# The end of an attention loop rearranged: one matmul group put back among the slots, casts moved to VectorE, gate sums moved into the loop

## The chip, the cores and the metric

The kernel runs on one core of a Trainium2 chip. The metric is the device time of the whole launch in microseconds, the median of several runs: 732.4 us before the change (three runs, 732.12 to 733.97 us). The profile is of one further execution, which took 732.09 us.

## The reference

With x of 2048 tokens by 512 features, everything in float32:

```python
g = sigmoid((x * gate_w).sum(-1, keepdims=True))      # one gate per token
q, k, v = x @ wqkv                                    # 32 heads of 16
p = softmax(mask(q @ k.T * 16 ** -0.5))               # causal, window of 256 keys
a = (p @ v) @ wo
b = (sigmoid(x @ w_gate) * (x @ w_up)) @ w_down       # hidden width 1376
return g * a + (1 - g) * b
```

## The kernel before, in words

Float32 products are made from parts. A value is split into a high part (a cast to the float32r type) and a low part (value minus high part), and a product is three matmuls: high by high, high by low, low by high. So each operand costs one cast (ScalarE, the function `split`, L84, and its relatives at L128 and L613) and one subtraction (VectorE, L85, L129, L614).

**First stretch, the attention loop.** The 32 heads form 8 groups of 4, a group has 16 blocks of 128 tokens, so there are 128 units (NU). The loop over `u` runs for N = 140 units, because a unit's later parts lag behind its first. In unit u the scores of block u are computed only for their row maxima (`s_part`, L338 on TensorE, L344 on VectorE, while u < 128), the transposed scores of block u - 9 are computed and exponentiated (`st_part`, L388 on TensorE, L393 on ScalarE, while u - 9 < 128), GpSimd masks them (`mask_p`, L398 and L403), and in some even units a burst of small matmuls multiplies probabilities by values (`pv_burst`, L442). The last bursts come in units 130, 132, 134, 136 and 138. What a burst gives is copied by ScalarE (L456), added to by VectorE (L459, `rest` in `o_take`) and stored to DRAM scratch, four stores of outputs and one of the softmax sums.

Between these parts stand **slots**. The generator `turns` walks through groups of 12 matmul steps: projections for later units, then the products with the gate and up weights (`gu_mm`, L271). A slot issues two half-height matmuls: step t of the chain on rows 0 to 63 and step t - 19 of the chain (SHIFT = 19) on rows 64 to 127. With G groups the chain has 12 G + 19 steps, of which the first and last 19 issue one half only. When a group ends, ScalarE copies it out of PSUM into a buffer with the tag `sp` (L548, four buffers), and its store to the scratch `gu_scratch` is queued. `run_slots(n)` takes n slots; the tables GAPS and LAST say how many follow each head hh, and LAST serves for u >= 128.

HOLD groups are left out of the chain and run at the end on the full array, 12 matmuls in one go (`hold_group`). Before the change HOLD is 1: the last group, up-projection chunk 10 for tokens 1536 to 2047, runs at the head of unit 138.

**Second stretch, the steps.** 44 steps n = (c, f), 4 token chunks of 512 by 11 hidden chunks, accumulate the down-projection: 4 token tiles by 3 matmuls, 12 in all (`pd`, L88 to L90). The third of each three (L90) needs the low part of the hidden values, the first needs the high part. After the last f of a chunk, 48 matmuls of the output projection (`pa`) follow, and the gate combines the two. The hidden values of a step are loaded from scratch five steps ahead (`h_load`, L627, two transfers of 256 KB), then `h_skew(n)` splits those of step n + 2 (L84, L85; tiles `hb`) and makes those of step n + 3 (sigmoid on ScalarE, L639; multiplication on VectorE, L640). `h_skew(-3)` to `h_skew(-1)` stand at the ends of units 136 to 138. There are seven buffers for loaded hidden values; those of steps 5 and 6 lie in memory that holds probabilities which the burst of unit 138 reads.

**What sets the order.** It is written out by hand: every engine works through its instructions in program order, and all transfers are issued by one queue, that of SyncE (called SPq in the profile), also in order. The lists `acts` and `behind` hold small jobs: after each head's matmuls one job of `behind` and one of `acts` is issued; a job of `acts` is a cast that puts its subtraction into `behind`. The list `later` holds stores that are issued at the head of the next unit. From unit 138 on (`u >= N - 2`) both lists are emptied at the end of the unit.

Other jobs at the loop's end: the down weights (`load_d`, `split_d`, tiles `wdraw` to `ring`), loaded every second unit from WD = 123 and split two units later; the output weights (`wo_split`, tiles `woraw` to `xh`, `xl`), put into `acts` in unit 136; and the inverses of the softmax sums (`sums_load`, L649, and `sums_invert`, L653), of which the fourth is loaded in unit 139 and inverted in step 2.

**The gate sums.** `z_load` loads a block of 128 tokens of x (tile `zx`, tag `sp`), `z_sum` multiplies it by the broadcast gate weights (`zw`) and sums along the row (L803). For the first chunk of tokens the loads stand in steps 0 and 1 and the sums in steps 2, 8 and 10.

Of the kernel before, what the change touches and what calls it, by code (L numbers as in the profile page):

```python
# [7 lines left out]
F32 = mybir.dt.float32  # L8
# [3 lines left out]
ALU = mybir.AluOpType  # L12
# [35 lines left out]
PVLAG = LAG + 2  # L48
SD = 3
QB = 32  # L50
HOLD = 1
GAP = 3
GAP0 = (4, 3, 5)
SHIFT = 19
GAPS = ((3, 3, 3, 3), (3, 2, 3, 0), (3, 3, 3, 3), (3, 2, 3, 2))
LAST = (3, 2, 3, 2)
WD_LATE = {0: 9, 2: 10}
WD_SPLIT = {0: 7, 1: 8, 3: 9, 5: 10}
AHEAD = 5


# [1 line left out]
def gated_mix_kernel(  # L63
# [60 lines left out]
    def split_d(f, late=False):  # L124
        fw = FCH[f]
        dh, dl = ring_f(f)
        hi, lo, raw = dh[0:fw], dl[0:fw], raw_d.pop(f)[0:fw]
        nc.scalar.copy(hi, raw)  # L128
        low = lambda: nc.vector.tensor_tensor(lo, raw, hi.bitcast(F32), op=ALU.subtract)  # L129
        behind.append(low) if late else low()  # L130

# [4 lines left out]
    with ExitStack() as actx:  # L136
# [473 lines left out]
            wo_raw.extend(raw[:, d] for d in range(2))  # L610

        def wo_split(d):
            nc.scalar.copy(wo_h[d], wo_raw[d])  # L613
            behind.append(lambda: nc.vector.tensor_tensor(  # L614
                wo_l[d], wo_raw[d], wo_h[d].bitcast(F32), op=ALU.subtract))

# [9 lines left out]
            for w in range(2):  # L626
                nc.sync.dma_start(hvs[n % NHV][0:FCH[f], w], gu_d[w, f, 0:FCH[f], c * CH:(c + 1) * CH])  # L627

        def h_skew(n):
            a, b = n + 2, n + 3  # L630
            if 0 <= a < len(steps):
                fw = FCH[steps[a][1]]
                hts[a] = cpool.tile([P, CH2], F32R, tag="hb", name=f"hb{a}", bufs=4)
                src = hvs[a % NHV][0:fw, 1]
                split(hts[a][0:fw, 0:CH], hts[a][0:fw, CH:], src)
            if 0 <= b < len(steps):
                fw = FCH[steps[b][1]]
                tg, tu = hvs[b % NHV][0:fw, 0], hvs[b % NHV][0:fw, 1]
                nc.scalar.activation(tg, tg, AF.Sigmoid)  # L639
                nc.vector.tensor_tensor(tu, tg, tu, op=ALU.mult)  # L640
# [16 lines left out]
            for _ in range(n):  # L657
                next(slots, None)

        def hold_group(step, _, post):  # L660
            for k in range(3 * ND):
                step(k)
            post()

        n_rest = len(work) + len(rest) + NSTEP - 8 - HOLD
        N = NU + PVLAG + 1
        SUMS = NU - 13 + PVLAG + 1
        U_LAST = 4 * (NSTEP - 2 - 5)
        HLOAD = N - 2 * AHEAD
        WD = NU - 5  # L670
        WO = NU - 8
        slots = turns()
        bursts = {}
        w = 0
# [6 lines left out]
        for u in range(N):  # L681
# [22 lines left out]
            later.clear()  # L704
            run_dmas(sdma[:SD])
            del sdma[:SD]
            if u in (WO, WO + 2):
                wo_load((u - WO) // 2)
            if u == N - 4:
                acts.extend(lambda d=d: wo_split(d) for d in range(ND))  # L710
            if WD <= u < WD + 18 and (u - WD) % 2 == 0:
                load_d((u - WD) // 2)
# [2 lines left out]
                s4 = (u + 2) // 4 + 4  # L715
            if s4 is not None:
                work.append(proj_group(s4))
            if u >= NU + PVLAG - HOLD and rest:
                hold_group(*rest.pop(0))
            for hh in range(HG):  # L720
                if hh == 0 and u % 2 == 0:
                    if u in bursts:
# [27 lines left out]
                        split_wqk(g, r, 0), behind.append(lambda: split_wqk(g, r, 1))))  # L750
            if 0 <= u - LAG < NU:
                mask_p(u - LAG)
            if WD + 2 <= u < WD + 16 and (u - WD) % 2 == 0:
                acts.append(lambda f=(u - WD) // 2 - 1: split_d(f, True))
            if SUMS <= u and (u - SUMS) % 4 == 0:
                sums_load((u - SUMS) // 4)
# [1 line left out]
                behind.append(lambda c=(u - SUMS) // 4: later.append(sums_invert(c)))  # L758
            if u >= HLOAD and (u - HLOAD) % 2 == 0:
                h_load((u - HLOAD) // 2)  # L760
            if u >= N - 2:
                flush(acts)
                flush(behind)
            if u >= N - 4:
                run_dmas(later)
                later.clear()
                if u < N - 1:
                    h_skew(u - N + 1)
        assert not (work or behind or acts or raw_gu or sdma or obs)

        def slot(h, d, c):
# [15 lines left out]
        wide = [blocks(spare[k][:, 2]) for k in range(2)]  # L787
        rows = [blocks(free_slot(0, k, 3)) for k in range(2)]
        accs = [spare[k % 2][:, k // 2] for k in range(4)]

        zx = {}
        zj = {}
        zw = cpool.tile([P, CH], F32, tag="ob", name="zw", bufs=2)
        nc.sync.dma_start(zw, gw.partition_broadcast(P).rearrange("p o f -> p (o f)"))

        def z_load(b):
            zx[b] = cpool.tile([P, CH], F32, tag="sp", name=f"zx{b}", bufs=4)
            nc.sync.dma_start(zx[b], x[b * P:(b + 1) * P, :])

        def z_sum(b, c):  # L800
            if c not in zj:
                zj[c] = ps.tile([P, D], F32, tag="st", name=f"zj{c}", bufs=3)
            nc.vector.tensor_tensor_reduce(  # L803
                zj[c], zx.pop(b), zw, scale=1.0, scalar=0.0, op0=ALU.mult, op1=ALU.add,
                accum_out=gsum[:, b:b + 1],
            )

        def gate(c):
            b = slice(4 * c, 4 * c + 4)
# [19 lines left out]
        for n, (c, f) in enumerate(steps):  # L829
            fw = FCH[f]  # L830
            if n + AHEAD < len(steps):
                h_load(n + AHEAD)
            h_skew(n)
            if n in WD_LATE:
                load_d(WD_LATE[n])
            if n in WD_SPLIT:
                split_d(WD_SPLIT[n])
            if f == 0:
                pd = [
                    ps.tile([P, D], F32, tag="s" if t < 2 else "st", name=f"pd{4 * c + t}", bufs=2 + t // 2)  # L840
                    for t in range(4)
                ]
            if n in (0, 1):
                z_load(2 * n)
                z_load(2 * n + 1)
            for b in {2: (0, 1), 8: (2,), 10: (3,)}.get(n, ()):
                z_sum(b, 0)
            if f == 8 and c + 1 < NC:
                for t in range(4):
                    z_load(4 * c + 4 + t)  # L850
            if f == NF - 1:
                gate(c)
            if n == 2:
                last_sums = sums_invert(NC - 1)
            if n == 3:
                nc.sync.dma_start(*last_sums)
            if 1 <= f < 9 and f % 2 == 1:
                o_load(4 * c + f // 2)
            if 3 <= f and f % 2 == 1:
                o_scale(4 * c + f // 2 - 1)  # L860
            if 4 <= f and f % 2 == 0:
                o_split(4 * c + f // 2 - 2)
            dh, dl = ring_f(f)
            hb = hts.pop(n)
            for t in range(4):
                ts = slice(t * P, (t + 1) * P)
                mm3(pd[t], hb[0:fw, ts], hb[0:fw, CH:][:, ts], dh[0:fw], dl[0:fw], f == 0, f == NF - 1)
            if f < NF - 1:
                continue
            for t in range(4):  # L870
                b = 4 * c + t
                acc = accs[b % len(accs)]
                nc.scalar.activation(acc, pd[t], AF.Copy, scale=omg[:, b:b + 1])
                pa = ps.tile([P, D], F32, tag="misc", name=f"pa{b}", bufs=3)
                for d in range(ND):
                    mm3(pa, oh[t][:, d], ol[t][:, d], wo_h[d], wo_l[d], d == 0, d == ND - 1)
                nc.vector.scalar_tensor_tensor(
                    acc, pa, gs[:, b:b + 1], acc, op0=ALU.mult, op1=ALU.add,
                )
                nc.sync.dma_start(out[b * P:(b + 1) * P, :], acc)  # L880
                if c + 1 < NC:
                    z_sum(b + 4, c)


_INS = ["xT", "wqk", "wv", "wo", "wgu", "wgu_last", "wg_last", "wd", "gw", "x"]
# [51 lines left out]
```

## Time and profile before

| what | value |
|---|---|
| time, median of three runs | 732.4 us |
| time of the profiled execution | 732.09 us |
| its span (first to last instruction) | 730.4 us |
| TensorE busy | 720.5 us, 99% |
| VectorE, ScalarE busy | 471.1 us, 436.8 us |
| TensorE's granted clock | 1.00 |
| bytes moved | 117.13 MB, mean 160 GB/s |

The span is 1.7 us shorter than the time of its execution; what lies around it is taken as fixed. The unit loop ends near 557 us of the span, where the burst of unit 138 ends; the 44 steps fill the rest. In rows of the timeline the columns are: start in us, duration in us, engine, line, operation, output and inputs, and in square brackets the idle time of the engine before it and who ended it. In rows of the chain they are start, duration, and what. Matmuls overlap: a full-width one is shown with 0.39 us, while the next starts 0.23 us after it.

### The profile page before, as it was taken

Reading aid. Unit: us, or ns where it says so; the run is one execution under the profiler, and the core shown is the slowest. Engines: PE = TensorE matmul, PEld = TensorE weight load, DVE = VectorE, ACT = ScalarE, POOL = GpSimd, SP = SyncE. Lnnn points to the kernel's source line nnn. Section 1 sums busy time; section 2 is a strip of 40 time slices with the busy share of each in tenths; the row PEclk is TensorE's granted clock in tenths of the full one; section 3 lists DMA queues with packets and bytes.
Section 4 is the critical chain, followed back from the end, with each engine's and each line's share of the span. In section 5 each row is a group of like instructions: output and inputs, shape, how many; then the busy total and the mean of one; then the engine's idle time right before and its main releaser. Section 6 shows DMA issues by size and latency. Waiting matters only on the chain.

```text
span 730.4 us, 20456 instructions
## 1 busy us (share of the span) xinstructions
PE 720.5 (99%) x7759; PEld 591.8 (81%) x7759; DVE 471.1 (65%) x1460; ACT 436.8 (60%) x899; POOL 166.8 (23%) x256
## 2 busy tenths in 40 slices
PE   9999999999999999999999999999999899999997
PEld 7688888888878878888787888888876688888886
DVE  5335766776676776767677676676426788577571
ACT  6412676677577666767667776766777455435241
POOL 7000332233223323323323323332321000000000
PEclk9999999999999999999999999999999999999999
DMA  9356455454355445445434635554466979567441
GB/s 321 98 155 205 121 134 150 140 144 127 121 137 149 132 136 142 131 136 136 136 115 139 160 86 150 166 151 153 124 203 177 304 260 274 185 228 244 155 131 58
DMA packets 88426, 117.13 MB, mean 160 GB/s; under 512 B 33294, under 2 KB 43150, under 8 KB 88328
## 3 DMA queue, kind: packets, MB, share of 16 engines
q1 hardware_dynamic: 88328, 115.83, 53.5%
q8 instruction: 61, 1.00, 0.6%
q14 instruction: 37, 0.30, 0.1%
HBM read 54.17 MB, written 36.45 MB: 124 GB/s over the span
## 4 chain that ended last, share of the span: by engine, by line
PE 93%; SPq 2%; DMA 2%; DVE 1%; ACT 1%; issue 0%; DVEq 0%; ACTq 0%
PE gu L271 36%; PE pj L271 10%; PE pvs L442 8%; PE st L388 6%; PE s L338 6%; PE pd L90 5%; PE pd L88 5%; PE pd L89 5%; PE vps L253 3%; PE pa L88 2%; PE pa L90 2%; PE pa L89 2%; SPq L313 2%; PE pvst L442 2%; PE gl L486 1%; PE vps L88 1%
## 5 line engine op out<-in xcount | busy, mean ns | idle before, releaser
L344 DVE CUSTOM_DVE_ANT_0 junk<-s,mask 128x384 f32<-128x384 f32 (+2 forms) x512 | 267.4, 531 | 150.7 <-PE st L388 89.3
L271 PE MATMUL gu<-xh,w 64*128 64x512 f32 x1280 | 337.2, 395 | 0.0
L393 ACT ACTIVATE region<-st 128x384 f32<-128x384 f32 (+2 forms) x512 | 241.7, 476 | 91.9 <-PE st L388 44.5
L271 PE MATMUL gu<-xl,w 64*128 64x512 f32 x640 | 228.9, 393 | 0.0
L271 PEld LDWEIGHTS gu<-xh,w 64*128 64x128 f32 x1280 | 190.5, 185 | 17.9 <-issue 5.5
L398 POOL TENSOR_SCALAR_AFFINE_SELECT region<-region 128x512 f32<-128x512 f32 x128 | 85.5, 668 | 367.0 <-ACT region L393 334.8
L388 PE MATMUL st<-ring 64*128 64x384 f32 (+2 forms) x536 | 168.1, 322 | 1.0 <-ACT region L393 0.6
L338 PE MATMUL s<-ring 64*128 64x384 f32 (+2 forms) x536 | 167.6, 321 | 0.3 <-DVE mx L344 0.3
L271 PEld LDWEIGHTS gu<-xl,w 64*128 64x128 f32 x640 | 115.0, 185 | 4.5
L338 PEld LDWEIGHTS s<-ring 64*128 64x128 f32 x536 | 98.6, 184 | 22.7 <-DVE mx L344 12.2
L388 PEld LDWEIGHTS st<-ring 64*128 64x128 f32 x536 | 98.3, 184 | 8.8 <-ACT region L393 1.9
L271 PE MATMUL pj<-xl,wqh 64*128 64x512 f32 (+1 forms) x240 | 95.5, 402 | 0.0
L271 PE MATMUL pj<-xh,wqh 64*128 64x512 f32 (+1 forms) x240 | 93.5, 394 | 0.0
L271 PE MATMUL pj<-xh,wql 64*128 64x512 f32 (+1 forms) x240 | 75.3, 392 | 0.0
L442 PE MATMUL pvs<-region,vg 64*32 64x320 f32 (+4 forms) x1440 | 73.4, 345 | 0.0
L90 PE MATMUL pd<-ring,hb 128*128 128x512 f32 (+1 forms) x176 | 69.4, 394 | 2.7 <-DVE hb L85 2.7
L403 POOL TENSOR_SCALAR_AFFINE_SELECT region<-region 128x512 f32<-128x512 f32 x112 | 71.9, 642 | 0.0
L442 PE MATMUL pvst<-region,vg 64*32 64x320 f32 (+4 forms) x1440 | 71.7, 340 | 0.0
L88 PE MATMUL pd<-ring,hb 128*128 128x512 f32 (+1 forms) x176 | 69.3, 394 | 0.7 <-ACT hb L84 0.7
L89 PE MATMUL pd<-ring,hb 128*128 128x512 f32 (+1 forms) x176 | 68.6, 390 | 0.0
L442 PEld LDWEIGHTS pvs<-region,vg 64*32 64x32 f32 x1440 | 45.2, 106 | 26.0 <-issue 5.5
L84 ACT CAST hb<-region 128x512 fp32r<-128x512 f32 (+1 forms) x37 | 23.0, 621 | 53.1 <-DVE region L640 43.9
(94 smaller groups left out, 1112.5 us busy)
## 6 DMA issues: line engine op xcount, KB each, us to landing
gu_scratch<-sp SPq DMA_DIRECT2D x80, 256.0 KB
region<-gu_scratch SPq DMA_DIRECT2D x68, 256.0 KB
ring<-sh SPq DMA_DIRECT2D x128, 128.0 KB
ring<-sl SPq DMA_DIRECT2D x64, 128.0 KB
guraw<-in_wgu_dram SPq DMA_DIRECT2D x20, 256.0 KB
v_scratch<-region SPq DMA_DIRECT2D x16, 272.0 KB
vg<-v_scratch SPq DMA_DIRECT2D x8, 544.0 KB
region<-in_xT_dram SPq DMA_DIRECT2D x16, 256.0 KB
```

The lines of the kernel that those rows point to most:

```text
L84: nc.scalar.copy(hi, src)
L88: mm(ps, lh, rh, start=first, stop=False)
L89: mm(ps, lh, rl, start=False, stop=False)
L90: mm(ps, ll, rh, start=False, stop=last)
L271: mm(pt[0:fw], (wl if w == 2 else wh)[r, d], (xl if w == 1 else xh)[r, d, c * CH:(c + 1) * CH], start=k == 0 and half != 1, stop=k == 3 * ...
L338: mm(pt[:, (k - k0) * P:(e - k0) * P], lhsT, blk(g, k, hh, 1, e - k), start=k == k0, stop=e == i + 1, skip_group_check=True,)
L344: nc.vector.tensor_tensor_reduce(junk[:, 0:n], pt[:, 0:n], mask[:, 3 * P - n:], scale=1.0, scalar=NEG, op0=ALU.add, op1=ALU.max, accum_out ...
L388: mm(pt[:, (q - j) * P:(e - j) * P], lhsT, blk(g, q, hh, 0, e - q), start=q == j, stop=e == last, skip_group_check=True,)
L393: nc.scalar.activation(pts[u][:, hh, 0:n], pt[:, 0:n], AF.Exp, scale=SCALE)
L398: nc.gpsimd.affine_select(p[:, :, 0:P], p[:, :, 0:P], pattern=[[0, HG], [1, P]], compare_op=ALU.is_ge, fill=0.0, base=0, channel_multiplie ...
L403: nc.gpsimd.affine_select(p[:, :, 2 * P:], p[:, :, 2 * P:], pattern=[[0, HG], [-1, P]], compare_op=ALU.is_gt, fill=0.0, base=0, channel_mu ...
L442: mm(acc[half][32 * hh:32 * hh + 32, q0:q1], vg[g % 2][r, c:c + 32], pts[g * NB + j][r, hh, q0 + o:q1 + o], start=m == 0, stop=m == len(or ...
```

## The change

Six things change, all near the end of the loop or just behind it:

1. HOLD and `hold_group` go. The last group joins the chain of slots.
2. LAST becomes (2, 2, 3, 2): nine slots per unit from unit 128 on, where there were ten.
3. The casts of the output weights (`wo_split`), of the down weights with f > 2 in the loop (`split_d` with `late`), and of the hidden values of steps 0 and 1 (`h_skew` inside the loop) are VectorE copies, where they were ScalarE's.
4. The output weights are split from unit 132 on (was 136). The down weights are loaded from unit 120 on (was 123), and split 7 moves from step 0 into the loop (unit 136).
5. The lists are emptied at the end of each unit from 136 on (was 138).
6. The gate sums of the first token chunk move: the broadcast weights are loaded in unit 123, the four blocks of x in units 126, 128, 130, 132, and the four sums are put into `behind` in units 128, 130, 132, 134. All gate sums now write their products over the x block, where they wrote into a PSUM tile.

```diff
-HOLD = 1
-LAST = (3, 2, 3, 2)
+LAST = (2, 2, 3, 2)
-WD_SPLIT = {0: 7, 1: 8, 3: 9, 5: 10}
+WD_SPLIT = {1: 8, 3: 9, 5: 10}
...
-        nc.scalar.copy(hi, raw)
+        (nc.vector.tensor_copy if late and f > 2 else nc.scalar.copy)(hi, raw)
...
         def wo_split(d):
-            nc.scalar.copy(wo_h[d], wo_raw[d])
+            nc.vector.tensor_copy(wo_h[d], wo_raw[d])
...
+                if by_vector:
+                    nc.vector.tensor_copy(hi, src)
+                    nc.vector.tensor_tensor(lo, src, hi.bitcast(F32), op=ALU.subtract)
+                else:
+                    split(hi, lo, src)
...
-        def hold_group(step, _, post):
-            for k in range(3 * ND):
-                step(k)
-            post()
-
-        n_rest = len(work) + len(rest) + NSTEP - 8 - HOLD
+        n_rest = len(work) + len(rest) + NSTEP - 8
...
-        WD = NU - 5
+        WD = NU - 8
...
+        def z_weight():
+            zw.append(wq_pool.tile([P, ND, P], F32, tag="wqh", name="zw").rearrange("p d f -> p (d f)"))
+            nc.sync.dma_start(zw[0], gw.partition_broadcast(P).rearrange("p o f -> p (o f)"))
+
+        def z_load(b):
+            zx[b] = cpool.tile([P, CH], F32, tag="sp", name=f"zx{b}", bufs=4)
+            nc.sync.dma_start(zx[b], x[b * P:(b + 1) * P, :])
+
+        def z_sum(b):
+            t = zx.pop(b)
+            nc.vector.tensor_tensor_reduce(
+                t, t, zw[0], scale=1.0, scalar=0.0, op0=ALU.mult, op1=ALU.add,
+                accum_out=gsum[:, b:b + 1],
+            )
...
+            if u == NU - 5:
+                z_weight()
+            if NU - 2 <= u < NU + 6 and u % 2 == 0:
+                z_load((u - NU) // 2 + 1)
+            if NU <= u < NU + 8 and u % 2 == 0:
+                behind.append(lambda b=(u - NU) // 2: z_sum(b))
-            if u == N - 4:
+            if u == N - 8:
                 acts.extend(lambda d=d: wo_split(d) for d in range(ND))
...
-            if u >= NU + PVLAG - HOLD and rest:
-                hold_group(*rest.pop(0))
...
-            if WD + 2 <= u < WD + 16 and (u - WD) % 2 == 0:
+            if WD + 2 <= u < WD + 18 and (u - WD) % 2 == 0:
                 acts.append(lambda f=(u - WD) // 2 - 1: split_d(f, True))
...
-            if u >= N - 2:
+            if u >= N - 4:
                 flush(acts)
                 flush(behind)
-            if u >= N - 4:
                 run_dmas(later)
                 later.clear()
                 if u < N - 1:
-                    h_skew(u - N + 1)
+                    h_skew(u - N + 1, True)
...
-            if n in (0, 1):
-                z_load(2 * n)
-                z_load(2 * n + 1)
-            for b in {2: (0, 1), 8: (2,), 10: (3,)}.get(n, ()):
-                z_sum(b, 0)
```

More of the change, by code (lines that the diff above doesn't have):

```diff
@@ L627, in h_load, with h_skew @@
                 nc.sync.dma_start(hvs[n % NHV][0:FCH[f], w], gu_d[w, f, 0:FCH[f], c * CH:(c + 1) * CH])
-        def h_skew(n):
+        def h_skew(n, by_vector=False):
             a, b = n + 2, n + 3
@@ L634, in h_skew @@
                 src = hvs[a % NHV][0:fw, 1]
-                split(hts[a][0:fw, 0:CH], hts[a][0:fw, CH:], src)
+                hi, lo = hts[a][0:fw, 0:CH], hts[a][0:fw, CH:]
+                if by_vector:
[3 more added lines that the diff above has]
+                    split(hi, lo, src)
             if 0 <= b < len(steps):
@@ L669, in gated_mix_kernel @@
         HLOAD = N - 2 * AHEAD
-        WD = NU - 5
+        WD = NU - 8
         WO = NU - 8
+        zx = {}
+        zw = []
+        def z_weight():
[10 more added lines that the diff above has]
+            )
         slots = turns()
@@ L789, in gated_mix_kernel @@
         accs = [spare[k % 2][:, k // 2] for k in range(4)]
[L791 to L806, printed above, removed]
         def gate(c):
@@ L881, in gated_mix_kernel @@
                 if c + 1 < NC:
-                    z_sum(b + 4, c)
+                    z_sum(b + 4)
 _INS = ["xT", "wqk", "wv", "wo", "wgu", "wgu_last", "wg_last", "wd", "gw", "x"]
```

## The prediction

> **What bounds the kernel now.** I read the page first.
>
> ```profile
> PE 720.5 (99%) x7759; PEld 591.8 (81%) x7759; DVE 471.1 (65%) x1460; ACT 436.8 (60%) x899; POOL 166.8 (23%) x256
> PE 93%; SPq 2%; DMA 2%; DVE 1%; ACT 1%; issue 0%; DVEq 0%; ACTq 0%
> ```
>
> TensorE (PE) sets the end, and its matmuls are the same before and after. A gain can only come from places where PE stands still, so I cut the span into stretches and looked for PE below its full 5 us. Behind the stretch follow the busy time of each engine, the granted clock, the DMA share and GB/s.
>
> ```profile
> 535.00:540.00 5.00, 4.77 (x94) 3.45 (x92) 1.12 (x2) 3.15 (x8) 1.22 (x2) 1.00 0.68 214
> 550.00:555.00 5.00, 4.38 (x78) 3.36 (x58) 2.49 (x4) 4.33 (x12) 1.55 (x2) 1.00 0.80 222
> 555.00:560.00 5.00, 3.88 (x75) 2.52 (x74) 3.73 (x7) 4.74 (x10) 0.00 (x0) 1.00 0.61 205
> 570.00:575.00 5.00, 3.04 (x14) 2.14 (x12) 3.59 (x8) 2.38 (x4) 0.00 (x0) 1.00 1.06 388
> 575.00:580.00 5.00, 4.69 (x19) 3.56 (x20) 4.63 (x9) 2.55 (x5) 0.00 (x0) 1.00 1.08 318
> ```
>
> The missing parts are 0.23, 0.62, 1.12, 1.96 and 0.31, together 4.24 us, all where the change works. PE's timeline names each wait:
>
> ```profile
> 551.03 0.32 PE L388 MATMUL st<-ring 64*128 64x128 f32 x1
> 551.61 0.50 PE L388 MATMUL st<-ring 64*128 64x128 f32 x2 [0.26 <-ACT ob L456]
> 552.48 0.32 PE L388 MATMUL st<-ring 64*128 64x128 f32 x1 [0.36 <-ACT region L393]
> 552.73 0.50 PE L271 MATMUL gu<-xh,wqh 128*128 128x512 f32 x1
> 557.66 0.50 PE L88 MATMUL pd<-ring,hb 128*128 128x512 f32 x1 [0.70 <-ACT hb L84]
> 558.82 0.50 PE L90 MATMUL pd<-ring,hb 128*128 128x512 f32 x1 [0.42 <-DVE hb L85]
> 575.02 0.50 PE L90 MATMUL pd<-ring,hb 128*128 128x512 f32 x1 [1.98 <-DVE hb L85]
> 578.34 0.51 PE L90 MATMUL pd<-ring,hb 128*128 128x512 f32 x1 [0.28 <-DVE hb L85]
> 591.78 0.39 PE L88 MATMUL pa<-xh 128*128 128x512 f32 x1
> 602.72 0.40 PE L88 MATMUL pd<-ring,hb 128*128 128x512 f32 x1
> ```
>
> The first four rows are unit 136: the slots ran out in unit 135, so its four small score products stand bare and wait for ScalarE. The next two are step 0 waiting for its hidden values, the two after that steps 5 and 6. The last two give the pace: 48 output matmuls in 602.72 - 591.78 = 10.94 us, 0.228 us each. The chain of waits says why step 5 is late:
>
> ```profile
> 561.47 1.69 DMA sum_scratch<-ob
> 563.54 1.14 SPq L794
> 566.15 5.88 DMA zx<-in_x_dram
> 572.06 0.70 DVE zj L803
> 572.86 0.70 DVE zj L803
> 573.62 0.53 DVE sm L653
> 574.34 0.63 DVE hb L85
> ```
>
> The queue waits 1.69 us for the last sums to land, issues the gate weights' broadcast (1.14), then x blocks. VectorE waits for an x block, makes two gate sums (two times 0.70 us and their read-outs) and an inverse, and only then the low part that step 5 has waited for since 573.04.
>
> **The change, part by part.** The sum is made against the profiled execution's 732.09 us, 0.31 below the median of 732.4.
>
> *The held group and nine slots.* The chain had 121 groups: 121 x 12 + 19 = 1471 steps, which by the tables end with the ninth slot of unit 135. With 122 groups it is 1483; at nine slots per unit from 128 they end with one slot in unit 138. Units 128 to 135 lose seven slots, units 136 to 138 gain 19, and 12 full-array matmuls go.
>
> ```profile
> 540.72 0.70 PE gu L271 x6
> 552.80 2.92 PE gu L271 x12
> ```
>
> Three slots (six halves) take 0.70 us, so 12 more slots cost 2.80 us against 2.92: nothing either way. What is gained is cover. Unit 136's products took 551.03 to 552.73, 1.70 us. Between slots, on the half of the array that a product uses, they add some 0.3 (an estimate: four 64x128 products, where 0.50 us is shown for two with their start). Gain 1.4 us.
>
> *Casts off ScalarE.* The 0.23 us at 539.81 comes from this chain:
>
> ```profile
> 537.88 0.41 ACT region L393
> 538.30 0.58 ACT ring L128
> 538.88 0.49 ACT sp L548
> 539.37 0.40 ACT region L393
> 539.81 0.44 PE st L388
> ```
>
> A cast of down weights stands between two exponentials, and PE waits for the second. The cast goes to VectorE: gain 0.25. Together the loop's end moves from 556.96 (557.66 less the wait of 0.70) by about 1.7 us, to 555.2.
>
> What a float32 cast costs on VectorE the trace doesn't show. The nearest rows:
>
> ```profile
> L128 ACT CAST ring<-wdraw x11: 601/611/627, 516.6 to 580.3; 128x512 fp32r<-128x512 f32 x10, 96x512 fp32r<-96x512 f32 x1
> L129 DVE TENSOR_TENSOR ring<-wdraw,ring x11: 627/684/693, 517.6 to 581.1; 128x512 fp32r<-128x512 f32 x10, 96x512 fp32r<-96x512 f32 x1
> 554.31 1.28 ACT L639 ACT_TABLE_LOAD   x1
> 559.29 0.42 DVE L459 TENSOR_TENSOR ob<-pvst,ob 128x256 f32<-128x256 f32 x1
> ```
>
> I take 0.68 us, the row on the same engine; half of it, 0.34, is the lower bound, with one source to read instead of two, and twice it, 1.4, the upper. Eleven casts (four output, five down, two hidden) are 7.5 us of VectorE in a stretch of the loop where it is busy at most 2.49 us of 5 before step 0. They hide there; at the upper bound they add 15 us to 30 and the last of them would be late.
>
> The Trainium skill, "VectorE: DVE Perf Modes", section "The perf-mode tier table (the rule you actually need)", says that a float32 copy from SBUF to SBUF runs at two elements per cycle where an operation with two tensors runs at one. By that rule step 0 would have its values some 0.35 us sooner, and the sum below would be 5.7 instead of 5.3. No run shown yet has such a copy.
>
> *Step 0.* Unit 136's last exponential ends near 551.4 (its products end 0.5 before the unit's slots, at 551.5). Then ScalarE loads its table (1.28) and makes the first sigmoid (0.63), to 553.4. VectorE follows in program order: product 0 (0.69) to 554.0, the third inverse (0.94, pitch 0.86) to 554.9, the cast (0.68, pitch 0.61) to 555.6, the low part to 556.2. PE, free at 555.2, waits 0.45 us for the first matmul and begins the third near 556.3 where it was 558.82. Gain up to this point 2.5 us, the 1.65 of above included. Emptying the lists two units sooner is what brings VectorE here with nothing else queued; it costs nothing, as PE has unit 137's slots to do. Step 1 needs its low part at 558.9; behind product 1 and unit 138's addition (0.42) VectorE has it near 558.4. That is the tightest place.
>
> *Gate sums.* From 558.82 to 591.78 PE issues 130 matmuls; at 0.228 that is 29.64 us, and 32.96 passed: 3.3 us lost, mostly to steps 5 and 6.
>
> ```profile
> 563.17 0.32 SPq L649 DMA_DIRECT2D sm<-sum_scratch  x1
> 564.78 0.84 SPq L627 DMA_DIRECT2D region<-gu_scratch  x2
> 570.00 0.63 ACT L639 ACTIVATE region<-region 128x512 f32<-128x512 f32 x1 [2.81 <-DMA region<-gu_scratch]
> ```
>
> After the change unit 138's addition, which ran at 559.29 behind hidden values, ends near 557.2. The four output stores (0.46 each), the wait of 1.69 and the load of the sums bring step 5's loads to about 561.0, as the broadcast and the x blocks are gone from between. With the 5.2 us that these loads took from issue to sigmoid (564.78 to 570.00, in the fullest stretch of the DMA, share 1.06), the sigmoid is at 566.2 and the low part at 569.2. Step 5 starts at 556.3 + 58 x 0.228 = 569.5. No wait. Gain 3.3, and if the loads stay as late as they were relative to PE, 1.6 (the two sums with read-outs).
>
> *In the loop* the sums cost VectorE 4 x 0.84 us and the queue five issues (1.14 and 4 x 0.45); both hide under PE's slots. The x blocks share four `sp` buffers with the groups' results: a result copied in units 128, 131, 132 and 136 takes the buffer of a block two to four units old. I cost that, and the three splits that move into units 122 to 127, at 0; a late block holds up ScalarE's copy and the exponentials behind it.
>
> *New waits.* With one slot fewer between the first two products after a burst, PE comes 0.23 us sooner to a buffer that ScalarE's copy frees. I take 0.5 us over all such places; bounds 0 and 2.5 (0.25 in each of ten units).
>
> Sum: 2.5 + 3.3 - 0.5 = 5.3 us; 732.09 - 5.3 = 726.8, and with part of the 0.31 that lies between this execution and the median, **727.0 us**.
>
> **Rivals.**
>
> *A. The loads stay the bound.* Step 5's buffers come free only with the last burst, and the stores before them are issued one by one. If the loads land 1.7 us later than I reckon, 1.7 - 0.3 of slack is lost in steps 5 and 6, and some of it again in step 7 with its shared DMA time: gain near 3.0, 729.1 us. For it: DMA shares of 1.06 and 1.08. Against it: the broadcast and four x blocks leave just that stretch.
>
> *B. The units become the bound.* With nine slots PE leaves ScalarE and VectorE 0.23 us less per unit. If each of ten units waits 0.25 us, the gain is 2.8: 729.3 us. For it: ScalarE is busy 3.15 to 4.33 of 5 us. Against it: the casts leave it.
>
> *C. The two together*, or VectorE's casts at their upper bound, so that step 0 starts as late as it did: gain near 0.8, 731.3 us, nothing to be measured.
>
> *D. Slower: late x blocks.* Queue and DMA at 0.68 to 0.80 bring a block so late that its sum isn't done when ScalarE needs the buffer. A block has some 8 us (two and a half units of 2.75 us and a burst); the longest chain row for one is 5.88. It decides above 8 us; at 10.2 each of the four costs 2.2 us, 8.8 against 5.3: 735.6 us. That block landed in the fullest stretch of all, so I give it little.
>
> *E. The masks.* GpSimd's last masks come 2 us before the burst that needs them:
>
> ```profile
> 550.17 0.63 POOL L398 TENSOR_SCALAR_AFFINE_SELECT region<-region 128x512 f32<-128x512 f32 x1 [0.99 <-ACT region L393]
> 553.92 0.91 POOL L398 TENSOR_SCALAR_AFFINE_SELECT region<-region 128x512 f32<-128x512 f32 x1 [3.12 <-ACT region L393]
> ```
>
> The second took 0.28 us more, beside a VectorE subtraction. If VectorE's new work holds up the last mask by two of its operations (1.36 us) and by as much two units earlier, bursts 136 and 138 each start 0.7 us late: gain 3.9, 728.2 us, inside the forecast's range. This is a rule of the Trainium skill, "SBUF — State Buffer", section "Who interferes with whom": VectorE and GpSimd take turns at a shared pair of ports, one blocks until the other is done. The 0.91 beside 0.63 agrees in its direction.
>
> **How the numbers follow.** Forecast 0.56, E 0.06, A 0.11, B 0.12, C 0.08, D 0.07. The forecast's own range is a gain of 3.9 to 6.8 (new waits 0, casts at 0.34, and the extra 0.1 us or so of a first matmul after each of the vanished waits): 725.3 to 728.2. With A and B the range reaches to 730.6. A difference under 0.3% (2.2 us, 730.2 to 734.6) can't be told from no change here. Faster: forecast, E, A and most of B, 0.83; same: C and the rest, 0.10; slower: D, 0.07.
>
> **What would show it.** Right: no bare score products in unit 136, no full-array `gu` matmuls, the first `pd` matmul near 555.6 with a short wait, step 5's loads issued near 561, no wait of PE from there to the last chunk, `zx` landing well before its sum. Wrong: PE waits for `region` (L393) or `ob` (L456) in units 128 to 137 (B); the sigmoid of step 5 after 568 (A); ScalarE's copy L548 waiting for `gsum` (D); bursts waiting for GpSimd (E); a VectorE cast far above 0.7 us (C).

## The result, and the profile after

The changed kernel takes 727.96 us (median of six runs, 726.99 to 729.04) against 732.26 us for the kernel before (six runs): a ratio of 0.9938 with a 95% interval of 0.9924 to 0.9953, 4.3 us or 0.6% faster. Forecast were 727.0 us and a range of 725.3 to 730.6. The profiled execution took 727.53 us with a span of 725.8 us. Of the executions below, one of `casts_act` took 1817.71 us and is left out of that kernel's ratio. Line numbers shift by a few; the down-projection's three matmuls are now L87 to L89.

The page of the changed kernel, engines' shares and the chain of waits:

```profile
PE 719.5 (99%) x7771; PEld 589.0 (81%) x7771; DVE 475.0 (65%) x1471; ACT 432.5 (60%) x888; POOL 168.0 (23%) x256
PE 96%; SPq 1%; ACT 1%; issue 0%; DVE 0%; DMA 0%; DVEq 0%
```

PE has three more points of the chain; the queue and the DMA gave them. The stretches that lost PE time before, and two that now do, 530 to 535 and 540 to 545 us (columns as before):

```profile
530.00:535.00 5.00, 4.79 (x44) 3.77 (x41) 3.14 (x6) 4.44 (x11) 1.51 (x2) 1.00 0.72 242
535.00:540.00 5.00, 4.96 (x95) 3.82 (x95) 3.20 (x9) 3.15 (x8) 1.36 (x3) 1.00 0.60 171
540.00:545.00 5.00, 4.87 (x93) 3.56 (x93) 5.00 (x9) 3.17 (x8) 3.39 (x4) 1.00 0.92 329
550.00:555.00 5.00, 5.00 (x56) 3.72 (x59) 1.56 (x4) 4.04 (x9) 0.63 (x1) 1.00 0.51 135
555.00:560.00 5.00, 4.58 (x62) 3.17 (x47) 4.93 (x9) 1.82 (x4) 0.00 (x0) 1.00 0.82 278
570.00:575.00 5.00, 5.00 (x23) 4.08 (x22) 4.06 (x8) 2.31 (x4) 0.00 (x0) 1.00 1.03 312
575.00:580.00 5.00, 5.00 (x23) 4.10 (x22) 4.58 (x10) 3.02 (x6) 0.00 (x0) 1.00 1.07 272
```

The waits of steps 5 and 6 (570 to 580 us) are gone, those of unit 136 (550 to 555) too. Step 0 still waits 0.41 us, and small losses of 0.21 and 0.13 us are new in the loop. Three marks on PE's timeline serve to measure every kernel below: the burst of unit 126, before the change's main work; the first L89 of step 0, the third matmul of a step (L90 before); and the first matmul of the second chunk.

```profile
512.90 0.43 PE L441 MATMUL pvs<-region,vg 64*32 64x320 f32 x1
556.77 0.50 PE L87 MATMUL pd<-ring,hb 128*128 128x512 f32 x1 [0.41 <-DVE hb L636]
557.50 0.50 PE L89 MATMUL pd<-ring,hb 128*128 128x512 f32 x1
598.33 0.40 PE L87 MATMUL pd<-ring,hb 128*128 128x512 f32 x1
```

Before, the same marks stood at 513.32, 558.82 and 602.72 us. So **stretch A**, from the burst to the first L89, took 45.50 us and now takes 44.60; **stretch B**, from there to the second chunk, took 43.90 and takes 40.83 (178 matmuls at 0.228 us would be 40.6). B gives 3.07 us, A 0.90. The remaining 0.6 of the 4.6 us of span lie ahead of the burst (0.42) and behind; the profiled executions of the different kernels have that first mark anywhere from 512.27 to 514.04 us.

### The profile page after: what moved, and what is told of

Its sections match the earlier page's. It is cut to its first block, busy times and chain, and to the rows that moved or that the text cites. A ratio compares the mean times of both kernels' runs of the same rounds, so it can differ in the third digit from the quotient of the medians.

```text
span 725.8 us, 20468 instructions
## 1 busy us (share of the span) xinstructions
PE 719.5 (99%) x7771; PEld 589.0 (81%) x7771; DVE 475.0 (65%) x1471; ACT 432.5 (60%) x888; POOL 168.0 (23%) x256
## 4 chain that ended last, share of the span: by engine, by line
PE 96%; SPq 1%; ACT 1%; issue 0%; DVE 0%; DMA 0%; DVEq 0%
PE gu L270 36%; PE pj L270 10%; PE pvs L441 8%; PE s L337 6%; PE st L387 6%; PE pd L87 6%; PE pd L89 6%; PE pd L88 6%; PE vps L252 3%; PE pa L87 2%; PE pa L89 2%; PE pa L88 2%; PE pvst L441 1%; SPq L312 1%; PE gl L485 1%; PE vps L87 1%
## 5 line engine op out<-in xcount | busy, mean ns | idle before, releaser
L392 ACT ACTIVATE region<-st 128x384 f32<-128x384 f32 (+2 forms) x512 | 242.4, 477 | 90.1 <-PE st L387 44.1
L87 PE MATMUL pd<-ring,hb 128*128 128x512 f32 (+1 forms) x176 | 69.3, 394 | 0.4 <-DVE hb L636 0.4
L89 PE MATMUL pd<-ring,hb 128*128 128x512 f32 (+1 forms) x176 | 69.1, 393 | 0.0
```

Source lines behind the costliest of these rows:

```text
L87: mm(ps, lh, rh, start=first, stop=False)
L89: mm(ps, ll, rh, start=False, stop=last)
L392: nc.scalar.activation(pts[u][:, hh, 0:n], pt[:, 0:n], AF.Exp, scale=SCALE)
```

## The experiments

All times are medians; ratios are against the kernel before on the same chip. A and B are read from each kernel's own profile at the three marks, so each is a single execution, which can lie up to 1 us from the median beside it. The shared runs of the kernel before had medians of 732.18, 732.40 and 732.32 us in the three groups.

| kernel | us | ratio, 95% interval | A | B |
|---|---|---|---|---|
| before | 732.26 | 1 | 45.50 | 43.90 |
| after | 727.96 | 0.9938 (0.9924 to 0.9953) | 44.60 | 40.83 |
| z_only | 727.79 | 0.9941 (0.9926 to 0.9956) | 45.47 | 41.01 |
| loop_only | 733.00 | 1.0015 (1.0005 to 1.0024) | 44.46 | 46.26 |
| add_sums | 727.94 | 0.9943 (0.9928 to 0.9958) | 44.61 | 41.95 |
| add_loads | 731.99 | 0.9993 (0.9982 to 1.0004) | 44.65 | 46.61 |
| late_inverse | 727.14 | 0.9926 (0.9911 to 0.9940) | 43.99 | 41.09 |
| gu_vec | 727.72 | 0.9937 (0.9920 to 0.9954) | 43.30 | 42.26 |
| ten_slots | 727.41 | 0.9935 (0.9917 to 0.9952) | 44.23 | 40.81 |
| casts_act | 730.07 | 0.9965 (0.9951 to 0.9979) | 46.76 | 40.83 |
| late_load | 726.64 | 0.9926 (0.9913 to 0.9940) | 43.95 | 40.77 |
| best | 726.13 | 0.9920 (0.9906 to 0.9933) | 43.18 | 40.69 |
| best_ten | 729.85 | 0.9966 (0.9956 to 0.9977) | 45.83 | 40.77 |

### The gate sums alone: z_only

The kernel before with part 6 of the change only.

```diff
+            if u == NU - 5:
+                z_weight()
+            if NU - 2 <= u < NU + 6 and u % 2 == 0:
+                z_load((u - NU) // 2 + 1)
+            if NU <= u < NU + 8 and u % 2 == 0:
+                behind.append(lambda b=(u - NU) // 2: z_sum(b))
...
-            if n in (0, 1):
-                z_load(2 * n)
-                z_load(2 * n + 1)
-            for b in {2: (0, 1), 8: (2,), 10: (3,)}.get(n, ()):
-                z_sum(b, 0)
```

> The kernel before with the gate sums of the first chunk moved into the loop and nothing else. If the loads and sums of the gate, standing ahead of steps 5 and 6, are what made PE wait there, those waits (1.98 and 0.28 us) and their restarts go: 3.0 to 3.3 us below the kernel before, about 729.1 us, with step 0 as late as before. If the gain comes from the loop's rearrangement, or if the chain of the last burst's stores alone keeps step 5 late, less than 1.5 us is gained.

It takes 727.79 us: all that the whole change gains, within the intervals. Its timeline of PE keeps both waits of step 0 and has none in steps 5 and 6:

```profile
557.01 0.50 PE L88 MATMUL pd<-ring,hb 128*128 128x512 f32 x1 [0.70 <-ACT hb L84]
558.16 0.50 PE L90 MATMUL pd<-ring,hb 128*128 128x512 f32 x1 [0.42 <-DVE hb L85]
599.17 0.40 PE L88 MATMUL pd<-ring,hb 128*128 128x512 f32 x1
```

B falls by 2.89 us and A by nothing. By the traces the whole change should be 1.05 us faster than this (0.87 in A, 0.18 in B). The times don't show it: the profiled execution here took 728.37 us, 0.58 above its median, and that of the changed kernel 0.43 below its own.

The queue and ScalarE show where the gain comes from (the loads of step 5, and its sigmoid):

```profile
564.07 0.84 SPq L627 DMA_DIRECT2D region<-gu_scratch  x2
566.85 0.63 ACT L639 ACTIVATE region<-region 128x512 f32<-128x512 f32 x1 [0.33 <-DMA region<-gu_scratch]
```

Counted from the burst of unit 126, these loads are issued after 51.38 us, and before the change after 51.46 (564.78 - 513.32): no sooner. But from issue to sigmoid they take 2.78 us in place of 5.22. With the broadcast and the x blocks gone the same loads land sooner; they don't start sooner.

### Everything but the gate sums: loop_only

The changed kernel with the code of that diff turned round.

> The changed kernel with the gate loads and sums of the first chunk put back into steps 0 to 10, as they were; the slots, casts and early splits stay changed. If the two parts add up, it keeps only what step 0 gained: 1.3 us below the kernel before, about 731.0 us, with the waits of steps 5 and 6 back. If the rearranged loop has already freed the queue early enough, step 5 waits less than 1 us and the time is below 729.5 us.

Slower than the kernel before by a little, 733.00 us (1.0005 to 1.0024), which neither half of the expectation foresaw. A keeps its gain (44.46), and B is 2.4 us longer than before the change:

```profile
573.09 0.50 PE L87 MATMUL pd<-ring,hb 128*128 128x512 f32 x1 [1.24 <-ACT hb L83]
575.84 0.51 PE L89 MATMUL pd<-ring,hb 128*128 128x512 f32 x1 [2.02 <-DVE hb L84]
```

PE comes to step 5 sooner, the data don't. The queue's timeline (stores of the groups' results, the last burst's stores, its sums, their load, the broadcast, step 5):

```profile
558.88 0.83 SPq L312 DMA_DIRECT2D gu_scratch<-sp  x2
559.80 2.75 SPq L312 DMA_DIRECT2D oT_scratch<-ob  x4
562.60 0.51 SPq L312 DMA_DIRECT2D sum_scratch<-ob  x1
564.30 0.34 SPq L653 DMA_DIRECT2D sm<-sum_scratch  x1
564.68 0.43 SPq L790 DMA_DIRECT2D zw<-in_gw_dram  x1
565.23 0.83 SPq L626 DMA_DIRECT2D region<-gu_scratch  x2
```

Step 5's loads are issued at 565.23, no sooner than before (564.78), though PE left the loop sooner. Unit 138's addition does start sooner (558.74; before 559.29), but the queue is busy with stores of the groups' results until 559.71, and the four stores of the burst then took 2.75 us where they took 1.69. Why they took longer isn't settled; they did so (2.50 to 3.32 us) in seven of the thirteen kernels here, in the changed kernel not (1.77). And the longer waits cost twice in this profile: the granted clock falls behind them.

```profile
576.00:579.00 3.00, 3.00 (x10) 2.37 (x11) 2.92 (x6) 1.43 (x3) 0.00 (x0) 0.73 1.07 298
579.00:582.00 3.00, 3.00 (x11) 2.37 (x10) 2.50 (x4) 2.00 (x4) 0.00 (x0) 0.70 1.08 352
582.00:585.00 3.00, 3.00 (x15) 2.47 (x14) 2.97 (x7) 1.88 (x3) 0.00 (x0) 1.00 1.10 250
```

Eight matmuls in a row, from 577.35 to 580.74 us, come some 0.42 us apart in place of 0.228: 1.6 us.

### One cost put back at a time: add_sums and add_loads

`add_sums` gives the changed kernel two gate sums in step 2 on VectorE, over the gate weights; their results go to a column that is written again later.

```diff
+            if n == 2:
+                zt = cpool.tile([P, CH], F32, tag="sp", name="zt", bufs=4)
+                for k in range(2):
+                    nc.vector.tensor_tensor_reduce(
+                        zt, zw[0], zw[0], scale=1.0, scalar=0.0, op0=ALU.mult, op1=ALU.add,
+                        accum_out=omg[:, NB - 1 - k:NB - k],
+                    )
```

> The changed kernel with two more VectorE gate sums in step 2 (over the gate weights, their result unused), where the sums of blocks 0 and 1 stood: 1.5 us of VectorE ahead of step 5's low part, without any load. In the changed kernel that low part ends near 569.1 us and PE needs it near 571.2, 2.1 us of slack: if the sums alone were what cost, PE waits again in step 5 for more than 1 us; if it took the late loads as well, nothing is lost (0 to 0.3 us, about 728.1 us).

`add_loads` gives it the broadcast and the four x blocks once more at their old places, into buffers that nothing reads.

```diff
+        zw2 = cpool.tile([P, CH], F32, tag="ob", name="zw2", bufs=2)
+        nc.sync.dma_start(zw2, gw.partition_broadcast(P).rearrange("p o f -> p (o f)"))
...
+            if n in (0, 1):
+                for k in (2 * n, 2 * n + 1):
+                    zt = cpool.tile([P, CH], F32, tag="sp", name=f"zt{k}", bufs=4)
+                    nc.sync.dma_start(zt, x[k * P:(k + 1) * P, :])
```

> The changed kernel with the broadcast and the four x blocks loaded once more in front of steps 0 and 1, where they stood, into buffers that nothing reads; no sums. Step 5's loads are issued 1.2 us later and share the DMA with 1.25 MB: if the transfers are the larger part of the price, its sigmoid comes 3 us or more later than in the changed kernel (565.9 us), PE waits 1 to 2 us in steps 5 and 6, about 729.5 us. If the price was the sums on VectorE, the transfers stay inside the 2.1 us of slack and the time is that of the changed kernel, about 728.0 us.

The sums alone: 727.94 us, the changed kernel's time, give or take the 1 us that the intervals leave; its profiled execution has one wait of 0.83 us in step 6 and a B that is 1.12 us longer. The loads alone: 731.99 us, the whole gain gone (0.9982 to 1.0004). ScalarE's and PE's timelines of `add_loads`:

```profile
569.41 0.63 ACT L643 ACTIVATE region<-region 128x512 f32<-128x512 f32 x1 [5.10 <-DMA region<-gu_scratch]
```

```profile
571.55 0.50 PE L87 MATMUL pd<-ring,hb 128*128 128x512 f32 x1 [0.88 <-ACT hb L83]
577.78 0.73 PE L89 MATMUL pd<-ring,hb 128*128 128x512 f32 x1 [2.04 <-DVE hb L84]
```

Step 5's loads were issued at 564.23 (562.73 in the changed kernel) and its sigmoid started 5.2 us later; in the changed kernel 3.2 us:

```profile
565.94 0.63 ACT L643 ACTIVATE region<-region 128x512 f32<-128x512 f32 x1 [1.23 <-DMA region<-gu_scratch]
```

Counted from the burst of unit 126 (at 512.45 here, 512.90 there), the sigmoid is 3.9 us late: the loads are issued 1.95 us later and take 2.0 us longer. Of the 1.95, 0.5 us are the broadcast and 1.4 us the last burst's four stores, which took 3.19 us here (1.77 there). These stores stand ahead of the added loads, so that part isn't known to be the loads' doing. It doesn't make the loss by itself: in `add_sums` the same stores took 2.89 us and step 5's loads were issued 1.1 us late, without a loss in the time. What cost before the change was the transfers; the sums on VectorE, which the chain of waits put beside them, cost at most about 1 us by themselves. What the sums cost while the loads are late, and which of the five transfers counts most, wasn't tried.

### The loop's parts: casts_act and ten_slots

`casts_act` puts nine casts back on ScalarE.

```diff
-        (nc.vector.tensor_copy if late and f > 2 else nc.scalar.copy)(hi, raw)
+        nc.scalar.copy(hi, raw)
...
-            nc.vector.tensor_copy(wo_h[d], wo_raw[d])
+            nc.scalar.copy(wo_h[d], wo_raw[d])
```

> The changed kernel with the casts of the output and down weights back on ScalarE (those of the hidden values stay on VectorE). If ScalarE sets the pace of the units, nine casts of 0.5 us between its exponentials in units 129 to 136 cost PE 1 to 2 us, about 729.2 us. If PE's waits there come from the order behind a burst alone, less than 0.5 us, about 728.2 us.

730.07 us, 2.1 us more, all of it in A (46.76, which is 1.26 more than before the change): casts on ScalarE do cost PE time, and with them there the loop's other changes are a loss in A. A wait of its timeline, 0.47 us where an exponential stands behind a cast and a copy:

```profile
540.85 0.44 PE L387 MATMUL st<-ring 64*128 64x384 f32 x1 [0.47 <-ACT region L392]
```

`ten_slots` goes back to ten slots, still with no group held.

```diff
-LAST = (2, 2, 3, 2)
+LAST = (3, 2, 3, 2)
```

> The changed kernel with ten slots per unit from unit 128 on, as before the change, still without a held group: the chain ends in unit 137. The groups then end at other heads than behind the bursts of units 130 and 134, so PE's waits there should go and burst 138 comes up to 0.9 us sooner; but unit 136 ends later against it, its last exponentials come about 0.4 us later, and step 0 waits 1 to 2 us for its values: about 728.3 us in sum. If the number of slots mattered by itself, as more work to cover ScalarE with, the time would be below 727.3 us.

727.41 us, between the two expectations and not to be told from the changed kernel. The trace has what was expected of the parts: PE fully busy from 530 to 545 us, the burst of unit 138 after 40.00 us from that of unit 126 (553.31 - 513.31; changed kernel 41.71), and then a long wait in step 0:

```profile
556.82 0.51 PE L87 MATMUL pd<-ring,hb 128*128 128x512 f32 x1 [1.73 <-DVE hb L636]
```

So the count of slots only moves the wait between the units and step 0.

### What step 0 waits for: late_inverse and gu_vec

`late_inverse` moves the third inverse of the sums, and its store, behind step 0's values.

```diff
-            if SUMS + 2 <= u and (u - SUMS) % 4 == 2:
+            if SUMS + 2 <= u < N - 3 and (u - SUMS) % 4 == 2:
...
+            if n == 1:
+                third_sums = sums_invert(NC - 2)
             if n == 2:
+                nc.sync.dma_start(*third_sums)
                 last_sums = sums_invert(NC - 1)
```

> The changed kernel with the third inverse of the softmax sums (and its store) moved from unit 137 to step 1. On VectorE it stood between step 0's product and its cast, 0.86 us on the chain that PE waits for before step 0 (0.41 us, and 0.16 us more before the first L89). If that chain is what ends step 0's wait, the wait goes or falls under 0.1 us and 0.4 to 0.6 us are gained, about 727.4 us; step 5's loads are issued up to 0.8 us sooner. If step 0 waits for something else, nothing moves.

Step 0's wait is gone (no idle time is shown before its first matmul), A falls by 0.61 us to 43.99; 727.14 us agrees with it, though its interval overlaps that of the changed kernel.

`gu_vec` copies the groups' results by VectorE from unit 128 on.

```diff
-            nc.scalar.copy(t, gp.pop((f, c, w)))
+            (nc.vector.tensor_copy if tail else nc.scalar.copy)(t, gp.pop((f, c, w)))
```

> The changed kernel with the groups' results copied out of PSUM by VectorE instead of ScalarE from unit 128 on. PE's new waits in units 130 to 134 (0.2 to 0.4 us each, before a transposed score product) are followed back to ScalarE, where such a copy stands between the burst's copy and the next exponential. If that order is the cause, these waits go, the burst of unit 138 starts 0.8 to 1.2 us sooner counted from the burst of unit 126, and the time falls to about 727.0 us. If ScalarE's exponentials alone are the bound, or VectorE's queue of casts holds the copies up, the same or more is waited.

The cause of the new waits was right: ScalarE's timeline of the changed kernel shows the copy (L547) between the burst's copy (L455) and the exponentials (L392), and PE waiting at 531.00.

```profile
529.47 0.59 ACT L455 COPY ob<-pvs 128x512 f32<-128x512 f32 x1 [2.34 <-PE pvst L441]
529.96 0.59 ACT L547 COPY sp<-gu 128x512 f32<-128x512 f32 x1
530.43 1.53 ACT L392 ACTIVATE region<-st 128x384 f32<-128x384 f32 x3
```

```profile
531.00 0.44 PE L387 MATMUL st<-ring 64*128 64x384 f32 x1 [0.21 <-ACT region L392]
```

Without it the burst of unit 138 comes 0.79 us sooner (40.92 us after that of unit 126; changed kernel 41.71), step 0's wait goes, and A is 1.30 us shorter (43.30). But B grows by 1.43, and the time stays at 727.72 us: PE arrives sooner than step 5's loads. The kernel takes all the late copies off ScalarE, so it doesn't tell a copy's place behind a burst from the lighter load.

```profile
569.57 0.51 PE L87 MATMUL pd<-ring,hb 128*128 128x512 f32 x1 [0.16 <-ACT hb L83]
573.77 0.50 PE L89 MATMUL pd<-ring,hb 128*128 128x512 f32 x1 [0.45 <-DVE hb L84]
```

### Both costs taken out together: late_load, best, best_ten

`late_load` keeps the late inverse and takes the load of the last sums, with its wait for their landing, out from ahead of the loads of steps 5 and 6.

```diff
-            if SUMS <= u and (u - SUMS) % 4 == 0:
+            if SUMS <= u < N - 1 and (u - SUMS) % 4 == 0:
...
+            if n == 1:
+                third_sums = sums_invert(NC - 2)
             if n == 3:
-                nc.sync.dma_start(*last_sums)
+                nc.sync.dma_start(*third_sums)
+                sums_load(NC - 1)
+            if n == 7:
+                last_sums = sums_invert(NC - 1)
+            if n == 8:
+                nc.sync.dma_start(*last_sums)
```

> The changed kernel with the third inverse in step 1 and with the load of the last sums behind step 3's other transfers (their inverse in step 7), so that the loads of steps 5 and 6 no longer stand behind the landing of the sums. Steps 5 and 6 already have slack in the changed kernel, so if PE has no other wait on the loads only the 0.4 to 0.6 us of the inverse are gained, as in the kernel that moves the inverse alone (about 727.2 us); the loads of step 5 are issued some 2 us sooner. If landing time was the limit anywhere behind step 5, more is gained.

`best` adds the copies of `gu_vec`:

```diff
-            nc.scalar.copy(t, gp.pop((f, c, w)))
+            (nc.vector.tensor_copy if tail else nc.scalar.copy)(t, gp.pop((f, c, w)))
```

> The kernel before this one, and the groups' results copied by VectorE from unit 128 on. The copies alone brought step 0's first L89 1.3 us forward, and steps 5 and 6 then waited 0.16 and 0.45 us (with their restarts about 0.8 us) for loads issued at 562.8 us. If the loads are that next bound, issuing them 2 us sooner keeps the 1.3 us, and with the inverse out of the way 1.6 to 1.9 us are gained on the changed kernel: about 726.2 us. If the DMA's landing time is the bound, the waits of steps 5 and 6 stay and it is 727.2 us.

`late_load` takes 726.64 us, step 5's loads are issued at 560.92; B is 40.77. `best` takes 726.13 us, ratio 0.9920 (0.9906 to 0.9933): no wait in step 0, none behind it, and stretches of 43.18 and 40.69 us.

```profile
555.34 0.51 PE L87 MATMUL pd<-ring,hb 128*128 128x512 f32 x1
555.92 0.39 PE L89 MATMUL pd<-ring,hb 128*128 128x512 f32 x1
596.61 0.40 PE L87 MATMUL pd<-ring,hb 128*128 128x512 f32 x1
```

Against the changed kernel's 727.96 that is 1.8 us less; the two ratios' intervals overlap in a narrow band (0.9924 to 0.9933), and the stretches A and B of the traces differ by 1.6 us. `best_ten` is the same with ten slots per unit:

```diff
-LAST = (2, 2, 3, 2)
+LAST = (3, 2, 3, 2)
```

> The same with ten slots per unit from unit 128 on. Ten slots brought the burst of unit 138 1.7 us forward and made step 0 wait 2.0 us for its values; with the inverse gone from that chain 0.9 us less. If the chain of table load, sigmoid, product and cast is what is left, it comes out near 726.7 us, step 0 waiting about 1 us; if the copies on VectorE free ScalarE enough that the last exponentials come sooner too, it equals the nine slots, 726.2 us.

729.85 us, 3.7 more than `best`, which nothing had forecast. With ten slots a group ends at the end of unit 133, just as the output casts and their subtractions fill VectorE. Its copy waits behind them, and PE, behind the burst of unit 134, waits for the PSUM buffer.

```profile
546.20 0.50 PE L270 MATMUL gu<-xh,wqh 64*128 64x512 f32 x1 [1.81 <-DVE sp L548]
```

```profile
544.43 1.11 DVE L614 TENSOR_TENSOR xl<-woraw,xh 128x512 fp32r<-128x512 f32 x1
545.47 0.68 DVE L548 COPY sp<-gu 128x512 f32<-128x512 f32 x1
```

The copy stood behind over 2 us of work on VectorE (the group's last matmul ends at 543.13), and A is 45.83 us, where `ten_slots`, with the copies on ScalarE, has 44.23.

## Why the prediction was right, and where it was off

The time lies in the range, and the largest term has the right size. Most of the way to it was otherwise than forecast.

**Gate sums (3.3 us): right in size, by two errors that cancel.** Stretch B gave 3.07 us, and `z_only` shows that this part alone gives the whole result in time. The sigmoid of step 5 was forecast at 566.2 and came at 565.94, but by luck. The prediction had the loads issued at about 561.0, and their 5.2 us to the sigmoid unchanged. They were issued at 562.73, 1.7 us after the forecast, and took 3.2 us:

```profile
562.73 0.84 SPq L626 DMA_DIRECT2D region<-gu_scratch  x2
```

The four stores ahead of them began at 558.77, not near 557.2, since unit 138's addition ended at 558.38 and stores of the groups' results held the queue until 558.68. And the prediction took the x blocks for transfers that delay these loads in the queue; before the change the first of them was issued at 566.15, behind the loads (564.78), and so couldn't delay their issue. The landing time, which the prediction held fixed, is what the removed transfers had cost: `z_only` shows 2.78 us with the loads issued as late as ever. For the two sums the prediction reckoned 1.6 us if the loads stayed late, and no run has that case: `z_only` takes the transfers away too, and in `add_sums` step 5's loads are there in time.

**The other five parts (2.0 us together): next to nothing.** Forecast were 2.5 up to the first L89 less 0.5 of new waits. The traces show 0.90 in A, the times nothing (727.96 against 727.79 us for `z_only`), and without the gate sums' move the same parts come out at 1.0015 times the kernel before (`loop_only`). The next two paragraphs say where it went.

**Held group and nine slots (gain 1.4), cast off ScalarE (0.25), new waits (0.5 lost): mis-sized.** PE was to be free for step 0 at 555.2 and was at 556.36 (556.77 less 0.41). Counted from the burst of unit 126 that is 43.46 us against 43.64 before (556.96 - 513.32): 0.2 us of gain in place of 1.15. Unit 136's bare products did vanish, but the new waits took it back: if the rest of the sum held, the term of 0.5 was nearer 1.5. The place named (first products after a burst) was right, the reason given (one slot fewer there) was not the whole of it: nine slots move the ends of groups, so that ScalarE copies a result right behind a burst. `gu_vec` gains 0.79 us up to the burst of unit 138 with such copies off ScalarE, all of them, wherever they stood. The cast's 0.25 was far too small in the other direction: `casts_act` shows 2.1 us for nine casts at nine slots. Of these, 0.5 us are step 0's longer wait (0.91), and 1.66 us come before the burst of unit 138, where its stretches of 5 us show only 0.4 us more of idle PE than the changed kernel's; how the rest is lost stays open. So the parts don't add up one by one.

**Step 0 (first L89 at 556.3): off by 1.2 us.** It came at 557.50, and counted from the burst of unit 126, which this execution reached 0.42 us sooner, it was off by 1.6. The chain was as forecast, but began later: the table load stands at 552.92 (forecast 551.4), as unit 136 ended later and a copy stood ahead of its last exponential. The rows of ScalarE and VectorE:

```profile
552.14 0.59 ACT L547 COPY sp<-gu 128x512 f32<-128x512 f32 x1 [0.41 <-PE st L387]
552.62 0.28 ACT L392 ACTIVATE region<-st 128x128 f32<-128x128 f32 x1
552.92 1.28 ACT L643 ACT_TABLE_LOAD   x1
```

```profile
554.88 0.69 DVE L644 TENSOR_TENSOR vg<-vg 128x512 f32<-128x512 f32 x1 [2.89 <-ACT vg L643]
555.49 0.95 DVE L657 RECIPROCAL sm<-sm 128x128 f32<-128x128 f32 x1
556.35 0.36 DVE L636 CAST hb<-vg 128x512 fp32r<-128x512 f32 x1
556.75 0.69 DVE L637 TENSOR_TENSOR hb<-vg,hb 128x512 fp32r<-128x512 f32 x1
```

The prediction saw the inverse (0.95) in that chain and left it there; `late_inverse` shows that it was worth 0.6 us of A. The cast on VectorE took 0.36 to 0.42 us undisturbed, near the lower bound (0.34) and not the 0.68 taken. The rule of the Trainium skill, "VectorE: DVE Perf Modes", section "The perf-mode tier table (the rule you actually need)", two elements per cycle for such a copy, agrees.

The sum was 5.3 us; the traces show 3.97 in the two stretches and the times 4.3.

**The rivals.** A's condition, loads 1.7 us later than reckoned, held for their issue; the shorter landing made up for it, so A is not what the changed kernel shows. It is the next bound: `gu_vec` ran into it as soon as PE came 1.3 us sooner. B, the units as the bound, is what ate the loop's gain, at a bit over half of the 2.5 us that the rival gave it, if the 1.5 above is right. C didn't happen. D, late x blocks, didn't either: no copy waited for a gate sum. E, masks held up, happened without harm (below).

## What to carry to other kernels

When a chain of waits runs through a transfer and then through the work on it, put each back alone before crediting either: here the work alone cost at most about 1 us, and the transfers beside the needed ones took the whole gain of 4. Ask of a load both when it is issued and how long it takes to land; taking other transfers away can shorten the second alone. Taking time out of a loop that feeds a queue gains nothing if the loads behind it start no sooner; `loop_only` came out slower with a shorter loop. And small jobs on an engine that a loop's matmuls wait for are dear: nine casts put back on ScalarE cost 2.1 us, and the late copies taken off it brought the last burst 0.79 us forward. Whether it is their place or their amount that costs, these runs don't separate.

## What the runs showed of the hardware

**A drop of the granted clock after waits of 1 to 2 us.** In `loop_only` PE waited 1.24 and 2.02 us with 0.7 us of matmuls between, and in `add_loads` 0.88 and 2.04 with some 4 us between. From 576 to 582 us the granted clock then read 0.73 and 0.70 in `loop_only`'s stretches of 3 us and 0.81 and 0.62 in those of `add_loads`, and matmuls came 0.43 us apart for some 3 us. The profile of the kernel before, with waits of 1.98 and 0.28 us, shows 1.00 around them. But that is one execution: in 33 of 49 others the kernel before had a mean clock of 0.996 to 0.998, as low as `loop_only` (0.997 to 0.998 in all ten), and five of the ten of `add_loads` had 0.999 or 1.00. So the drop followed waits of this size in both of these profiles, and these runs don't show what decides whether it comes. The Trainium skill, "TensorE: Matmul & The Clock Gate", section "Why this matters for your kernels", asks for no idle gap above about 3 us between matmul bursts; here the clock fell behind gaps of 0.88 and 2.04 us, and the measurement decides.

**VectorE and GpSimd hold each other up.** GpSimd's masks take 0.63 to 0.64 us in the quiet part of the loop. In the changed kernel, while VectorE makes the output casts, they and VectorE's own operations grow:

```profile
542.23 1.05 POOL L397 TENSOR_SCALAR_AFFINE_SELECT region<-region 128x512 f32<-128x512 f32 x1 [0.93 <-ACT region L392]
543.24 1.08 POOL L402 TENSOR_SCALAR_AFFINE_SELECT region<-region 128x512 f32<-128x512 f32 x1
```

```profile
540.74 1.11 DVE L613 TENSOR_TENSOR xl<-woraw,xh 128x512 fp32r<-128x512 f32 x1
542.71 1.12 DVE L128 TENSOR_TENSOR ring<-wdraw,ring 128x512 fp32r<-128x512 f32 x1
```

A subtraction of 0.69 us takes 1.11 and a mask 1.05 to 1.08, some 0.4 us more for each meeting. The Trainium skill, "SBUF — State Buffer", section "Who interferes with whom", has the two engines share a pair of ports, one blocking until the other is done; the trace agrees with it. No burst of the changed kernel waited for it.
